# A convolution and maxout kernel: w10 from 16 products, four columns first added on VectorE, sums of one batch moved ahead

## Chip, cores, metric

One core of a Trainium2 chip. The sets of experiments (a; b and c; d to g) ran on three different chips, so kernels of different sets are compared by their ratios and not by their medians. Times are device microseconds (us) of a whole execution. A profiled execution also has a span, which is 1.8 us shorter than its time. Each kernel was timed in alternation with the kernel before on the same chip. A ratio is the mean time of one kernel's fast runs over that of the other's fast runs of the same rounds, so it is not quite the ratio of the medians quoted.

## The reference, cut to what matters

```python
w = softmax(weight_gen, over the 7 taps)          # 8 batches x 4160 rows x 8 heads x 7
y[b,s,h,g] = sum_k w[b,s,h,k] * x_pad[b,s+k,h,g]  # 7 taps, 24 values per head, 192 columns
h1 = y @ w1;  h2 = y @ w2                         # 192 -> 1024
out = maximum(h1, h2) @ w_out                     # 1024 -> 192
```

The kernel uses max(h1, h2) = h1 + relu(h2 - h1): `out = y @ (w1 @ w_out) + relu(y @ (w2 - w1)) @ w_out`. The small product `w10 = w1 @ w_out` is made once, at the start.

## The kernel before

The 33,280 rows are laid out as 260 columns of 128 rows. VectorE multiplies x by the seven weights and adds the taps (`mul`, `adds`). For the first columns TensorE does the adding, by seven products with an identity; for the others a transposing DMA brings the sum to TensorE.

```python
    def adds(b, o):
        ...
        nc.vector.tensor_tensor(out=taps(0, 1, 3), in0=taps(0, 1, 3), in1=taps(3, 1, 3), op=ALU.add)
        nc.vector.tensor_tensor(out=taps(0, 2, 2), in0=taps(0, 2, 2), in1=taps(1, 5, 2), op=ALU.add)
        nc.vector.tensor_tensor(out=y_ts[b][:, o * D:(o + w) * D], ...)

    def transpose(u):
        ...
        nc.sync.dma_start_transpose(out=yt[...], in_=y_ts[b][:, o * D:(o + n) * D])
        ...
            nc.gpsimd.tensor_copy(out=gate, in_=yt[:, 0:1])   # waits for the transpose, then loads x

    def sum_transpose(u):
        for k in range(nb):
            for t in range(K):                                # seven taps
                nc.tensor.matmul(yps[...], lhsT=m_ts[b][...], rhs=ident, start=(t == 0), stop=(t == K - 1), ...)
        nc.scalar.copy(out=yt[:, 0:nb * P], in_=yps[:, 0:nb * P])
```

Eight columns are a unit here. Each unit passes VectorE (product, three adds), a transpose, TensorE (`hd`, products with w2 - w1), ScalarE (`rd_t`, the relu), TensorE again (`op_ps`), ScalarE (`o_t`, the copy out) and a store.

The softmax here doesn't subtract the row's maximum and nothing guards it: scores larger than these inputs give would overflow.

## Time and profile before

428.1 us (427.99 to 428.15, three runs); with the fourth run beside the changed kernel (427.70) the median is 428.05.

| | before |
|---|---|
| span | 425.9 us |
| TensorE busy | 418.4 us, 98% |
| VectorE busy | 381.8 us, full from 30 us to 391.4 us |
| transposes of w1, products of w10 | 2.58 us, 1.98 us |
| last copy out starts, end | 422.16, 425.9 us |

The lines of the page and how they are read are in the prediction below. The end of the kernel before is shown here: the timeline of ScalarE (ACT), with start, duration, engine, line and what ended the idle time.

```profile
422.16 0.48 ACT L305 COPY o_t<-op_ps 128x384 f32<-128x384 f32 x1 [1.01 <-PE op_ps L292]
422.67 0.34 ACTq L312 DMA_DIRECT2D out_dram<-o_t  x1
```

One copy of the last two columns waits for TensorE, then one store follows; 3.74 us from the copy's start to the end.

### The profile page before, as it was taken

To read this page: it belongs to the slowest core of one execution; us is meant where nothing else is said; L and a number is where in the kernel's file an instruction comes from. 1 tells how busy PE (TensorE), PEld (TensorE's weight loads), DVE (VectorE), ACT (ScalarE), POOL (GpSimd) and SP (SyncE) were. 2 spreads that over 40 slices of the span, in tenths; PEclk is the share of its full clock that TensorE was granted. 3 is DMA by queue.
4 is the path that set the end of the run, shared out by engine and by line. 5 is a ranking of instruction groups with operands and counts; after the bars stand their busy time and mean duration, and the time that the engine had idled before them with its cause. 6 is when DMAs were issued, how large, how long until landed. Compare 5 with 4: busy or idle time off the path is not lost.

```text
span 425.9 us, 9277 instructions
## 1 busy us (share of the span) xinstructions
PE 418.4 (98%) x4139; PEld 300.2 (70%) x4139; DVE 381.8 (90%) x176; ACT 351.5 (83%) x353; POOL 81.5 (19%) x101
## 2 busy tenths in 40 slices
PE   7999999999999999999999999999999999999996
PEld 7889876666776767766667767667666677676685
DVE  6989999999999999999999999999999999997000
ACT  5896889898888979788898979898887988787762
POOL 1510032323112213221201131130222113110000
PEclk9999999999999999999999999999999999999999
DMA  8994256585675656667776667666766566644112
GB/s 253 252 233 93 76 145 150 86 198 168 169 191 112 202 130 184 159 130 192 175 193 124 161 159 184 138 165 179 178 154 182 96 162 149 154 115 131 75 75 111
DMA packets 62167, 65.85 MB, mean 155 GB/s; under 512 B 49937, under 2 KB 50577, under 8 KB 62128
## 3 DMA queue, kind: packets, MB, share of 16 engines
q0 software_dynamic: 8128, 24.11, 27.0%
q1 hardware_dynamic: 48672, 15.59, 18.7%
q10 hardware_dynamic: 5328, 25.56, 15.4%
q8 instruction: 32, 0.52, 0.5%
q14 instruction: 7, 0.06, 0.0%
HBM read 35.96 MB, written 25.56 MB: 144 GB/s over the span
## 4 chain that ended last, share of the span: by engine, by line
PE 94%; ACT 3%; DMA 2%; SPq 1%; issue 0%
PE op_ps L292 40%; PE hd L237 27%; PE hd L247 14%; PE op_ps L282 5%; PE op_ps L275 3%; PE yps L208 2%; DMA xs<-in_x_dram 2%; PE hdp L237 1%; ACT rd_t L256 1%; PE hdp L247 1%; PE tp L490 1%; SPq L426 1%; PE pw L533 0%; ACT en_t L146 0%; ACT o_t L305 0%; ACT xb_t L455 0%
## 5 line engine op out<-in xcount | busy, mean ns | idle before, releaser
L256 ACT ACTIVATE rd_t<-hd 128x2048 bf16<-128x2048 f32 (+1 forms) x166 | 230.9, 1445 | 33.1 <-PE hd L247 32.6
L292 PE MATMUL op_ps<-wo,rd_t 128*128 128x192 bf16 x2080 | 200.2, 246 | 0.0
L157 DVE TENSOR_TENSOR m_t<-xb_t,en_t 128x10752 bf16<-128x10752 bf16 (+1 forms) x36 | 187.3, 5206 | 1.7 <-ACT en_t L146 1.5
L292 PEld LDWEIGHTS <-rd_t 128*128 128x128 bf16 x2080 | 175.6, 98 | 9.2
L192 POOL CAST gate<-yt 128x1 f32<-128x1 bf16 x28 | 45.8, 1635 | 278.9 <-DMA yt<-y_t 278.9
L237 PE MATMUL hd<-yt,wdE 128*128 128x512 bf16 (+1 forms) x264 | 96.5, 370 | 0.2 <-ACT rd_t L256 0.2
L237 PE MATMUL hd<-yt,wdO 128*128 128x512 bf16 (+1 forms) x264 | 95.5, 366 | 0.0
L175 DVE TENSOR_TENSOR m_t<-m_t 128x4608 bf16<-128x4608 bf16 (+1 forms) x31 | 76.9, 2480 | 1.1
L305 ACT COPY o_t<-op_ps 128x384 f32<-128x384 f32 (+1 forms) x89 | 56.1, 630 | 25.9 <-PE op_ps L292 23.8
L247 PE MATMUL hd<-yt,wdR 64*128 64x512 bf16 (+1 forms) x528 | 68.0, 366 | 0.0
L282 PE MATMUL op_ps<-w,yt 128*128 128x192 bf16 x260 | 64.0, 246 | 0.0
L176 DVE TENSOR_TENSOR m_t<-m_t 128x3072 bf16<-128x3072 bf16 (+1 forms) x31 | 52.9, 1706 | 1.1
L247 PEld LDWEIGHTS <-wdR 64*128 64x128 bf16 x576 | 20.8, 94 | 44.8 <-issue 35.0
L237 PEld LDWEIGHTS <-wdE 128*128 128x128 bf16 x288 | 28.0, 97 | 29.0 <-issue 19.2
L146 ACT ACTIVATE en_t<-wg_t 128x896 bf16<-128x896 f32 (+1 forms) x36 | 34.2, 960 | 2.1 <-ACT o_t L305 2.1
L237 PEld LDWEIGHTS <-wdO 128*128 128x128 bf16 x288 | 28.2, 98 | 10.4 <-issue 0.7
L282 PEld LDWEIGHTS <-yt 128*128 128x128 bf16 x260 | 25.4, 98 | 9.6 <-issue 0.3
L177 DVE TENSOR_TENSOR y_t<-m_t 128x1536 bf16<-128x1536 bf16 (+1 forms) x31 | 28.9, 932 | 1.1
L275 PE MATMUL op_ps<-w,yt 64*128 64x192 bf16 x260 | 25.2, 243 | 0.2 <-ACT o_t L305 0.2
L275 PEld LDWEIGHTS <-yt 64*128 64x128 bf16 x260 | 12.8, 94 | 14.6 <-issue 0.7
L130 DVE TENSOR_REDUCE sum_t<-e_t 128x128 f32<-128x896 f32 (+1 forms) x17 | 17.6, 1038 | 2.3 <-ACT e_t L125 2.3
L125 ACT ACTIVATE e_t<-wg_t 128x896 f32<-128x896 f32 (+1 forms) x17 | 15.7, 925 | 3.9 <-DMA wg_t<-in_weight_gen_dram 2.3
(51 smaller groups left out, 161.7 us busy)
## 6 DMA issues: line engine op xcount, KB each, us to landing
out_dram<-o_t ACTq DMA_DIRECT2D x29, 768.0 KB, 3.8
xb_t<-in_x_dram POOLq DMA_DIRECT2D x28, 384.0 KB, 4.7
wg_t<-in_weight_gen_dram POOLq DMA_DIRECT2D x14, 448.0 KB, 5.1
xb_t<-xb_t POOLq DMA_DIRECT2D x16, 288.0 KB, 5.0
out_dram<-o_t ACTq DMA_DIRECT2D x6, 384.0 KB, 2.6
wg_t<-in_weight_gen_dram SPq DMA_DIRECT2D x2, 448.0 KB, 5.2
xs<-in_x_dram SPq DMA_DIRECT2D x2, 384.0 KB, 6.4
xb_t<-in_x_dram POOLq DMA_DIRECT2D x1, 768.0 KB, 10.4
```

The costliest lines, as they stand in the source:

```text
L146: nc.scalar.activation(out=_sub(en_ts[b], o * WGC * 2, [[2 * N, K], [2, N], [1, 2]]), in_=_sub(wg_ts[b], o * WGC, [[1, K], [K, N], [0, 2]] ...
L157: nc.vector.tensor_tensor(out=m_ts[b][:, K * o * D:K * (o + n) * D], in0=_sub(xb_ts[b], o * D, [[D, K], [1, n * D]]), in1=_sub(en_ts[b], o ...
L175: nc.vector.tensor_tensor(out=taps(0, 1, 3), in0=taps(0, 1, 3), in1=taps(3, 1, 3), op=ALU.add)
L176: nc.vector.tensor_tensor(out=taps(0, 2, 2), in0=taps(0, 2, 2), in1=taps(1, 5, 2), op=ALU.add)
L192: nc.gpsimd.tensor_copy(out=gate, in_=yt[:, 0:1])
L237: nc.tensor.matmul(hid_out(t, f, j), lhsT=wd[kind][:, f * P:(f + 1) * P], rhs=_sub(yt_ts[u], 2 * j * P, [[3 * P, w // P], [1, P]]), start= ...
L247: nc.tensor.matmul(hid_out(t, f, j), lhsT=wd["R"][r, f * P:(f + 1) * P], rhs=_sub(yt_ts[u][r, :], P, [[3 * P, w // P], [1, P]]), start=fir ...
L256: nc.scalar.activation(out=rd[:, k * 1024:(k + n) * 1024], in_=hd[:, at:at + n * 1024], func=AF.Relu)
L275: nc.tensor.matmul(op_out(c), lhsT=yt_ts[u][r, (3 * i + 1) * P:(3 * i + 2) * P], rhs=w10[r, 2 * D:3 * D], start=first, stop=False, skip_gr ...
L282: nc.tensor.matmul(op_out(c), lhsT=yt_ts[u][:, (3 * i + 2 * j) * P:(3 * i + 2 * j + 1) * P], rhs=w10[:, j * D:(j + 1) * D], start=False, s ...
L292: nc.tensor.matmul(op_out(c), lhsT=rd[:, k * 1024 + at:k * 1024 + at + P], rhs=wo[:, f * D:(f + 1) * D], start=False, stop=(f == FCH - 1), ...
L305: nc.scalar.copy(out=_sub(o_t[0], (k + 2 * q) % 24 * D, [[2 * D, w], [D, 2], [1, D]]), in_=_sub(tile_, at + q * D, [[D, w], [512, 2], [1, ...
```

## The change

It takes transposes and products off TensorE while w10 is made, has VectorE do the first of the adding steps of columns 16 to 19 so that TensorE sums four taps instead of seven, brings the softmax sums of batch 1 ahead of the last product of batch 0, splits the last copy and store over two engines, and moves later softmax work by a few tiles.

```diff
+        nc.vector.tensor_tensor(out=taps(0, 1, 3), in0=taps(0, 1, 3), in1=taps(3, 1, 3), op=ALU.add)
+        if first:
+            return
 ...
-            for t in range(K):
+            for t in taps:
 ...                                                     # in evac, for the last pair
+            for j, copy, eng in ((0, nc.scalar.copy, nc.scalar), (1, nc.vector.tensor_copy, nc.sync)):
+                copy(out=o_t[0][...], in_=tile_[:, at + j * 512:at + j * 512 + D])
+                eng.dma_start(...)
 ...                                                     # transposes of w1
-                for at, kind, nr in ((0, "E", P), (P + 64, "E", 64), (P, "T", 64)):
+                for at, kind, nr in ((0, "E", P), (P, "T", 64)):
 ...                                                     # the order
         mul(0, 8)
         sum_transpose(1)
-        mul(0, 12)
         exp_sum(1)
         red(1)
         hidden(1)
-        w1_transposed()
         ln(1)
         shift(1)
+        mul(0, 12)
+        w1_transposed()
+        weights(1, 0)
+        weights(1, 4)
 ...                                                     # w10
-            for k in range(3):
+            for at, c0, nr in ((0, 0, P), (512, P, 64)):
                 for fi in range(FCH):
                     nc.tensor.matmul(...)
-            nc.scalar.copy(out=_sub(w10, 0, [[D, 3], [1, D]]), in_=_sub(pw, 0, [[256, 3], [1, D]]))
+            for k, to, frm, at in ((0, 0, 0, 0), (1, 0, 64, 0), (2, 64, 0, 0), (1, 64, 0, 512), (2, 0, 0, 512)):
+                nc.scalar.copy(...)
 ...
         mul(1, 0)
+        adds(1, 0, True)
 ...
-        4: (lambda: (exp_sum(3), sum_transpose(4)), lambda: weights(2, 0)),
+        4: (lambda: (exp_sum(3), sum_transpose(4, (0, 1, 2, K - 1))), lambda: weights(2, 0)),
 ...
-        if s == 1 and b + 2 < NB:                        # ln, shift, mul, adds of later batches
+        if s == 4 and b + 2 < NB:
```

## The prediction

> **What bounds the kernel now.** I read the page's busy times and forty slices first, then the chain that ended last, then the timeline of each engine, then the landings of the transposing DMA.
>
> ```profile
> PE 418.4 (98%) x4139; PEld 300.2 (70%) x4139; DVE 381.8 (90%) x176; ACT 351.5 (83%) x353; POOL 81.5 (19%) x101
> ...
> PE   7999999999999999999999999999999999999996
> ...
> DVE  6989999999999999999999999999999999997000
> ...
> PE 94%; ACT 3%; DMA 2%; SPq 1%; issue 0%
> ```
>
> TensorE (PE) is busy from 3.0 us to the end, and 94% of the chain is TensorE. The reader should also see the DVE row: VectorE is full from 30 us until it has finished at 391.4 us. In the DVE timeline one half batch (8 columns) takes 12.05 us (y_t written at 61.60, 73.65, 85.69 us); in the PE timeline the first products of units three apart (131.06 and 167.11 us) lie 36.05 us apart, 12.02 us per half batch. So TensorE is the bound, but VectorE keeps exactly its pace, only some microseconds ahead of it.
>
> How far ahead is what limits this change. GpSimd's gate waits for each transpose, so its start shows the landing; I compare it with TensorE's first product on that unit.
>
> ```profile
> 189.46 1.88 POOL L192 CAST gate<-yt 128x1 f32<-128x1 bf16 x1 [11.76 <-DMA yt<-y_t]
> 210.06 2.77 POOL L192 CAST gate<-yt 128x1 f32<-128x1 bf16 x1 [7.77 <-DMA yt<-y_t]
> 246.18 2.78 POOL L192 CAST gate<-yt 128x1 f32<-128x1 bf16 x1 [8.17 <-DMA yt<-y_t]
> 298.11 1.62 POOL L192 CAST gate<-yt 128x1 f32<-128x1 bf16 x1 [12.00 <-DMA yt<-y_t]
> ```
>
> The first column is the start. TensorE needs these units at 190.9, 213.3, 249.4 and 299.0 us: slacks of 1.4, 3.2, 3.2 and 0.9 us. Of 28 units most have 2.5 to 3.3 us, some 4 to 5; the first and fourth above are the smallest. (The gate at 298.11 may overstate: the last data packets of that transpose ended 2 us before.)
>
> Between 20 and 45 us, where most of the change is:
>
> ```profile
> 23.21 1.93 ACT L496 COPY w1t<-tp 128x1024 bf16<-128x1024 bf16 x2 [0.52 <-PE tp L490]
> 31.39 0.69 ACT L539 CAST w<-pw 128x576 bf16<-128x576 f32 x1
> 25.38 1.09 DVE L138 TENSOR_TENSOR wg_t<-wg_t,sum_t 128x896 f32<-128x896 f32 x1 [0.64 <-ACT sum_t L133]
> 27.71 2.96 DVE L157 TENSOR_TENSOR m_t<-xb_t,en_t 128x5376 bf16<-128x5376 bf16 x1 [1.24 <-ACT en_t L146]
> 28.51 2.14 PE L533 MATMUL pw<-wo,w1t 128*128 128x192 bf16 x24
> 37.79 2.51 PE L208 MATMUL yps<-ident,m_t 128*128 128x128 bf16 x42
> 45.10 0.27 PE L237 MATMUL hd<-yt,wdE 128*128 128x256 bf16 x1 [0.23 <-ACT rd_t L256]
> ```
>
> ScalarE (ACT) has no gap from 23.2 to 32.1 us, VectorE has two, and TensorE waits 0.23 us for ScalarE at 45.1 us and 0.20 us at 50.8 us, then never again before the tail.
>
> **What the Trainium skill says.** "TensorE: Matmul & The Clock Gate", "Wait — 56ns, not 53.3ns?": back to back, a product costs its columns at 2.4 GHz plus about 2.5 ns, 55.6 ns for 128. The trace agrees: 42 products of 128 columns take 2.35 us (56 ns), 24 of 192 columns take 1.98 us (82.5 ns). "TensorEngine Tiling (Array Packing)", "Key Properties": changing the tiling mode drains TensorE. The trace agrees: among the transposes of w1 the weight loads come 0.15 us apart where 128 rows change to 64 or back, 0.03 us apart between two of 64 rows. "DMA: Bandwidth & Descriptors", "Issuing engines are not separate DMA queues": issuing from two engines saves only issue time; no run here shows it yet for the last store. The same page, "Queues, rings and completion order": a semaphore increment lands only after every earlier write of that DMA engine, across queues. The trace fits: where an output store is issued 0 to 1.15 us after y_t is ready, transposes land 5.7 to 7.7 us after it; where it comes 1.23 us or more after, 3.9 to 4.75 us.
>
> **The change part by part.**
>
> 1. *Transposes of w1, 24 to 16.* Before, eight chunks take 20.53 to 23.11 us, 0.32 each: two mode changes of 0.15 and one load of 0.03. The new pair keeps both mode changes, so only 8 x 0.03 = 0.25 us goes, not a third of 2.6.
> 2. *w10 products, 24 to 16.* 8 x 82.5 ns = 0.66 us; eight have 64 weight columns, which changes the tiling mode once or twice (estimate 0.1 us back). About 0.6 us.
> 3. *Copies on ScalarE.* w1t copies shrink by 2 x 256 elements at 0.83 ns (the slope between 384 and 768 elements, 0.48 and 0.80 us): -0.43 us. w10's one copy of 0.69 us becomes five of 192; back to back a copy costs its elements plus some 0.05 us (1024 elements start 0.905 us apart), so 0.21 each with 0.33 for the last: about +0.5 us. ln ahead of w1t fills the 0.52 us idle. Walking ScalarE's order with these starts, w10 is ready at 31.7 us; TensorE, 0.8 us early, asks for it at 32.1 us. No stall, but only 0.4 us to spare.
> 4. *Columns 16 to 19.* Four taps instead of seven: 18 of 42 products, 18 x 56 ns = 1.0 us off TensorE. VectorE gets one add of 1.36 us (what the same shape takes at 34.57 us). It ends at about 31.2 us and is asked for at 37.0 us: hidden.
> 5. *Sums of batch 1 ahead of the last product of 0.* Fills most of the two VectorE gaps: reduction at 20.9, subtraction 22.9 to 24.0, then products without waiting. The second product of batch 1 moves from 31.58 to about 32.15 us: 0.56 us later, the 1.4 us add less 0.8 us of gap. From there VectorE has no idle, so all its later work is 0.56 us later.
> 6. *Last pair.* Intended: two engines copy and two queues store. But the built program's waits show otherwise: ScalarE's copy waits for the last product of both columns and VectorE's copy waits for ScalarE's. So 0.33 + 0.3 us in a row (estimates) take the place of 0.48; the store is 96 KB instead of 192, worth some 0.15 us (192 KB land in 2.1, 384 in 2.6 us). Net 0, at worst +0.2.
> 7. *Later places* of ln, subtraction, weights: VectorE's order is unchanged, ScalarE's work the same. The tightest, the weights of batch 3, would be ready at about 73 us for a product at 75.1 us. Nothing.
>
> Sum on TensorE: 0.25 + 0.6 + 1.0 = 1.85 us. At 42 to 45 us ScalarE is on the chain: its order (copy of yt, copy out, weights, relu) can come forward by 1.5 us, where the copy of yt ends. So TensorE is 1.5 us early from 45 us on. It does not wait again in the trace before, so this carries to the end if nothing new waits: 428.1 - 1.5 = 426.6.
>
> **The rivals.**
>
> *A, it carries through*: 426.6 us. For it: 94% of the chain, no later waits; and where a store is issued just after y_t, moving it to well before y_t should shorten those landings, among them the two tightest.
>
> *B, VectorE and the transposes become the bound.* TensorE and the stores it sets off move 1.5 us forward, VectorE 0.56 us back: 2.1 us against slacks of 0.9 to 3.3. If no landing changes its latency, the unit at 299.0 us waits 1.2 us, and 0.3 us of gain is left: 427.8. A variant: for every third unit the store now comes 3.0 to 3.6 us after y_t; 2.1 less puts the late ones (from 242 us) under 1.15 us, where landings took 2 us longer, and 3.0 - 2.1 - 2.3 is a wait of 1.4 us: 428.0. Against it: the same shift takes the two tightest units out of the bad place.
>
> *C, ScalarE with five copies holds TensorE up at 32 us.* If each copy costs 0.33 us alone, w10 is ready at 32.2 to 32.4 us: 0.1 to 0.3 us lost, 426.9. And a *better A*, where the waits of 45 and 51 us go too: 1.85 + 0.4, 425.8.
>
> **Range and chances.** A about half, B or a part of it a third, C and the better A the rest. The middle of these is 426.8 us; 8 in 10 between 425.7 and 428.0. A change of 2% is 8.6 us; all the TensorE work touched is under 3 us, and the worst wait found is under 3, so within 2% gets 0.98, and 0.01 each side.
>
> **What would show it.** The page: PE products fewer by 34 (8 + 8 + 18). The transposes of w1 still about 2.3 us; the 16 products about 1.4 us; 24 products near 37 us in 1.34 us; no wait at op_ps near 32 us; first hd product of 256 columns near 43.6 us. VectorE's y_t of the first half batch at about 50.1 us. ScalarE's and VectorE's last copies one after the other. Under A no unit's first product waits for a transpose; under B the waits show one of 0.3 us or more for yt, and all TensorE time after it shifts. Wrong would be: a transposing pair well under 0.3 us, VectorE later by over 1 us, or TensorE idle above 1 us between 60 and 400 us.

## The result, and the profile after

The changed kernel took 427.0 us (426.37 to 427.49, four runs) against 428.05: ratio 0.9976, 95% interval 0.9959 to 0.9993. Six runs of a later set gave 426.79 us (426.52 to 426.95), ratio 0.9968. The profiled execution is the fastest of the first four, 426.37 us.

The page of the changed kernel: busy times, the slices of TensorE and VectorE, the chain by engine.

```profile
PE 416.6 (98%) x4105; PEld 298.2 (70%) x4105; DVE 383.6 (90%) x178; ACT 352.1 (83%) x357; POOL 89.7 (21%) x101
...
PE   7999999999999999999999999999999999999996
...
DVE  6999999999999999999999999999999999999000
...
PE 92%; ACT 4%; DMA 2%; SPq 1%; issue 1%; ACTq 0%; DVE 0%; DVEq 0%
```

34 products fewer, 1.8 us less of TensorE, two instructions and 1.8 us more on VectorE, whose dip between 21 and 32 us (the third slice) is gone. The timelines between 20 and 45 us:

```profile
23.09 1.50 ACT L508 COPY w1t<-tp 128x768 bf16<-128x768 bf16 x2
30.66 1.56 ACT L555 CAST w<-pw 128x192 bf16<-128x192 f32 x5
24.04 5.82 DVE L157 TENSOR_TENSOR m_t<-xb_t,en_t 128x5376 bf16<-128x5376 bf16 x2
29.89 1.36 DVE L173 TENSOR_TENSOR m_t<-m_t 128x2304 bf16<-128x2304 bf16 x1
28.39 1.60 PE L547 MATMUL pw<-wo,w1t 128*128 128x192 bf16 x16
37.23 1.50 PE L210 MATMUL yps<-ident,m_t 128*128 128x128 bf16 x24
43.85 0.27 PE L239 MATMUL hd<-yt,wdE 128*128 128x256 bf16 x1 [0.54 <-ACT rd_t L258]
```

ScalarE's copies, the add, the 16 and the 24 products stand where the prediction put them to some 0.3 us, except that the five copies end at 32.2 us and not at 31.7. TensorE now waits 0.54 us for ScalarE at 43.85 us, where it had waited 0.23. The ends, in the timelines of ScalarE, VectorE and the queue of SyncE:

```profile
420.85 0.32 ACT L307 COPY o_t<-op_ps 128x192 f32<-128x192 f32 x1 [1.00 <-PE op_ps L294]
421.26 0.36 DVE L307 COPY o_t<-op_ps 128x192 f32<-128x192 f32 x1 [29.28 <-ACT o_t L307]
421.65 0.36 SPq L308 DMA_DIRECT2D out_dram<-o_t  x1
```

VectorE's copy is released by ScalarE's copy and not by TensorE: the two run one after the other, and from 420.85 us to the end of the span (424.6) it is 3.75 us, as long as before.

The landings of the transposes, seen in GpSimd's gate (start first):

```profile
165.41 2.42 POOL L194 CAST gate<-yt 128x1 f32<-128x1 bf16 x1 [11.21 <-DMA yt<-y_t]
176.23 1.04 POOL L194 CAST gate<-yt 128x1 f32<-128x1 bf16 x1 [7.40 <-DMA yt<-y_t]
186.69 2.64 POOL L194 CAST gate<-yt 128x1 f32<-128x1 bf16 x1 [8.40 <-DMA yt<-y_t]
295.67 2.05 POOL L194 CAST gate<-yt 128x1 f32<-128x1 bf16 x1 [8.98 <-DMA yt<-y_t]
```

TensorE needs these units (its first weight load for them is due) at 165.8, 175.9, 189.6 and 297.7 us. The third and fourth are the two that were tightest before: they have 2.9 and 2.0 us now. The first two have 0.4 and -0.3 us: a weight load waited 0.3 us there, which TensorE's queued work hid. Over the 28 units the median slack fell from 2.84 to 1.66 us.

**Four stretches.** Four marks in TensorE's timeline cut an execution into parts that answer to different causes: the first transpose of w1, the first product `hd`, the start of the last eight products, the end of the span. All times in us; the last two columns are the median of the timed runs and the ratio to the kernel before.

| kernel | to transposes of w1 | to first hd | to last eight | to end | median | ratio |
|---|---|---|---|---|---|---|
| before | 20.53 | 24.57 | 376.20 | 4.60 | 428.05 | 1 |
| changed | 20.64 | 23.21 | 376.14 | 4.61 | 427.0 | 0.9976 |
| a1_again | 20.78 | 23.21 | 376.52 | 4.59 | 426.79 | 0.9968 |
| a2_vector_less | 20.27 | 23.23 | 376.13 | 4.57 | 426.27 | 0.9957 |
| a3_vector_more | 20.77 | 23.20 | 379.90 | 4.53 | 428.13 | 1.0001 |
| a4_vector_twice | 20.37 | 24.18 | 378.28 | 4.57 | 430.19 | 1.0057 |
| b1_seven_taps | 20.52 | 23.90 | 376.14 | 4.54 | 427.15 | 0.9984 |
| b3_old_w10 | 21.11 | 24.18 | 376.15 | 4.56 | 427.41 | 0.9989 |
| b5_old_order | 21.58 | 23.40 | 377.23 | 4.59 | 427.89 | 0.9998 |
| c1_own_banks | 20.35 | 23.21 | 376.93 | 4.41 | 427.14 | 0.9984 |
| d1_sums_earlier | 20.68 | 23.19 | 376.13 | 4.60 | 426.39 | 0.9963 |
| e1_exp_later | 20.38 | 22.90 | 376.67 | 4.55 | 427.21 | 0.9995 |
| g1_store_later | 20.67 | 22.95 | 380.44 | 4.64 | 430.89 | 1.0072 |
| f1_all | 21.08 | 22.94 | 376.48 | 4.40 | 426.59 | 0.9962 |

The last of the four is good to 0.05 us only, since the spans are given to 0.1 us. Each ratio has a 95% interval of 0.0012 to 0.0029 to either side, so ratios that differ by less than some 0.002 are not told apart by the times.

The first column scatters by over 1 us between executions of kernels that do the same there up to that point, or nearly so; differences of 0.3 us between single spans say nothing for that reason. The second column is the gain of the change: 24.57 - 23.21 = 1.36 us. The third is 376.13 to 376.20 us in every execution without a wait there; what is above that is waits and what they set off, and in c1 and f1 also a moved product of 0.26 us. The table has one profiled execution of each kernel, the medians come from four to seven.

### The profile page after: what moved, and what is told of

Read it like the earlier page. It is cut to its first block, busy times and chain, and to the rows that moved or that the text cites. A ratio compares the mean times of both kernels' runs of the same rounds, so it can differ in the third digit from the quotient of the medians.

```text
span 424.6 us, 9214 instructions
## 1 busy us (share of the span) xinstructions
PE 416.6 (98%) x4105; PEld 298.2 (70%) x4105; DVE 383.6 (90%) x178; ACT 352.1 (83%) x357; POOL 89.7 (21%) x101
## 4 chain that ended last, share of the span: by engine, by line
PE 92%; ACT 4%; DMA 2%; SPq 1%; issue 1%; ACTq 0%; DVE 0%; DVEq 0%
PE op_ps L294 39%; PE hd L239 27%; PE hd L249 14%; PE op_ps L284 5%; PE op_ps L277 3%; DMA xs<-in_x_dram 2%; PE yps L210 2%; ACT rd_t L258 2%; PE hdp L239 1%; PE tp L502 1%; PE hdp L249 1%; SPq L437 0%; ACT en_t L146 0%; ACT o_t L316 0%; ACT yt L216 0%
## 5 line engine op out<-in xcount | busy, mean ns | idle before, releaser
L194 POOL CAST gate<-yt 128x1 f32<-128x1 bf16 x28 | 54.7, 1955 | 272.4 <-DMA yt<-y_t 272.4
L173 DVE TENSOR_TENSOR m_t<-m_t 128x4608 bf16<-128x4608 bf16 (+1 forms) x32 | 78.2, 2445 | 1.1
```

## The experiments

### How much VectorE can be late

a1_again is the changed kernel. a3 and a4 add one or two adds of the same size on dead taps; a2 leaves the new add out (its four columns are wrong; relative error 0.075).

```diff
         if first:
+            nc.vector.tensor_tensor(out=taps(3, 1, 3), in0=taps(3, 1, 3), in1=taps(3, 1, 3), op=ALU.add)   # a3; twice in a4
             return
```

```diff
-        nc.vector.tensor_tensor(out=taps(0, 1, 3), in0=taps(0, 1, 3), in1=taps(3, 1, 3), op=ALU.add)       # a2
         if first:
             return
+        nc.vector.tensor_tensor(out=taps(0, 1, 3), in0=taps(0, 1, 3), in1=taps(3, 1, 3), op=ALU.add)
```

> The changed kernel unaltered, as the base for the others of this call and to see how far its executions scatter. Theory B (VectorE and the transposes hold TensorE up in some executions): 426.9 us median, and a scatter of about 1 us against 0.4 us for the kernel before. Theory A (TensorE's work alone): the executions agree within 0.4 us, near 426.5.

> The add of 1.36 us on VectorE is left out and TensorE still sums only four taps, so four columns come out wrong on purpose; TensorE's work is the same and VectorE is 1.36 us earlier from 31 us on. Theory A: the time of the changed kernel within 0.1 us. Theory B: 0.4 to 0.7 us faster, near 426.4, and the scatter falls to 0.4 us or less.

> A second add of the same 1.36 us on taps that nobody reads again follows the first; results stay right, TensorE's work is the same, VectorE is 1.36 us later from 31 us on. Theory A: the time of the changed kernel within 0.2 us. Theory B: 0.7 to 1.4 us slower, 427.6 to 428.3, with TensorE waiting for a transpose in the trace.

> Two such adds, VectorE 2.72 us later. Theory A with 2 us of slack left: 0.7 us slower than the changed kernel at most. Theory B: 2.0 to 2.7 us slower, 429.0 to 429.7, since each us of VectorE past the slack is a us of the end.

Measured on one chip: 426.27 (VectorE 1.36 us earlier), 426.79 (as changed), 428.13 (1.36 later), 430.19 us (2.72 later). TensorE's work is the same in all four, so the time follows VectorE: less steeply while there is slack left, by 0.5 us from a2 to a1, by 1.3 us from a1 to a3 and by 2.1 us from a3 to a4, each a step of 1.36 us. a4 is 0.5 us above the range expected of it (429.0 to 429.7); two of its six runs had a lower granted clock, see below. The scatter of a1 was 0.43 us and not 1, that of a2 (0.60) not smaller, and that of the kernel before 1.8 us in the same set and not 0.4: that part of the expectation failed, and scatter is no sign of the waits. In the waits of a1 there was this:

```profile
PEld L249 <- DMA yt<-y_t: 0.7, 1, 0.7
...
PE hd L249 <- DMA yt<-y_t: 0.2, 1, 0.2
```

Columns: total us, times, longest. One weight load waited 0.7 us for a transpose and TensorE 0.2 us. In a2 no such wait is listed, and its third stretch is 0.39 us shorter. The unit waited for is the one needed at 176 us, and it is the same unit that is waited for in c1, e1 and b5 below. It landed 5.7 to 6.6 us after its y_t in these executions, while most others whose store comes at the same place landed after 4.0 to 4.7 us; why this one is slow is open.

a3's profiled execution (430.22 us, its slowest) showed more than was looked for. In TensorE's timeline, and below it four stretches from 104 to 112 us (busy times of the engines, then the granted clock PEclk):

```profile
106.32 0.39 PE L250 MATMUL hd<-yt,wdR 64*128 64x512 bf16 x2 [1.93 <-ACT rd_t L259]
```

```profile
104.00:106.00 2.00, 0.39 (x4) 0.00 (x0) 2.00 (x1) 1.64 (x2) 0.00 (x0) 1.00 0.70 133
106.00:108.00 2.00, 1.68 (x14) 1.14 (x15) 1.97 (x2) 0.86 (x2) 1.25 (x3) 0.84 0.00 0
108.00:110.00 2.00, 2.00 (x15) 1.90 (x13) 1.97 (x2) 0.47 (x1) 0.00 (x0) 0.50 0.88 88
110.00:112.00 2.00, 2.00 (x21) 1.93 (x19) 1.97 (x3) 0.00 (x0) 0.00 (x0) 0.80 0.95 257
```

The wait is put down to ScalarE, but a weight load just before waited 2.4 us for the transpose: that unit landed 6.57 us after y_t. After the idle 1.93 us the granted clock fell to half. From the shares 0.84, 0.50 and 0.80 the fall began at about 107.4 us, 1.0 us after the wait had ended, and lasted 3.4 us. So the wait cost twice: the third stretch is 3.8 us over its floor (376.14 us). In a4 two gaps came without a fall of the clock:

```profile
44.55 0.27 PE L241 MATMUL hd<-yt,wdE 128*128 128x256 bf16 x1 [1.51 <-ACT rd_t L260]
106.94 0.39 PE L251 MATMUL hd<-yt,wdR 64*128 64x512 bf16 x2 [1.59 <-DMA yt<-y_t]
```

The first of them is in its second stretch: TensorE waited for ScalarE, which stood behind the later VectorE.

The record has the mean granted clock of every run, profiled or not. 3.4 us at half clock lower it by 0.004 (estimate: 3.4 / 2 / 428). It is 0.998 or more in every profiled run without such a fall, and 0.996 in a3's slowest run. The other runs at 0.996 or less are a4's two slowest, e1's slowest and all six of g1: those lost time to the clock too.

### The parts undone

```diff
-        adds(1, 0, True)                                     # b1_seven_taps
-        4: (lambda: (exp_sum(3), sum_transpose(4, (0, 1, 2, K - 1))), ...
+        4: (lambda: (exp_sum(3), sum_transpose(4)), ...
```

> Columns 16 to 19 are summed from seven taps on TensorE again and VectorE's add of 1.36 us is gone; all else as changed. TensorE has 18 products (1.0 us) more, of which 0.54 us falls into its present wait for ScalarE at 43.9 us, and VectorE is 1.36 us earlier. By TensorE's work alone: 0.5 to 1.0 us slower than the changed kernel, 427.3 to 427.8. With VectorE's lead deciding part: the waits for transposes go, so about 427.1 to 427.3, as good as the changed kernel within 0.4 us, and with a small scatter.

427.15 us, inside the second expectation. In the profile its second stretch is 0.69 us longer than the changed kernel's (1.0 us of products, of which 0.3 went into a shorter wait for ScalarE) and the third stands on its floor: with VectorE 1.36 us earlier no transpose was waited for. The add that saves TensorE 0.7 us takes from VectorE's lead.

```diff
-                for at, kind, nr in ((0, "E", P), (P, "T", 64)):             # b3_old_w10: w10 as before
+                for at, kind, nr in ((0, "E", P), (P + 64, "E", 64), (P, "T", 64)):
 ...                                                          # and 24 products, one copy
```

> Transposes, products and copies of w10 as before (24, 24, one copy), all else as changed. In the profiles the new ones saved 0.23 us of transposes and 0.44 us of products. By TensorE's work alone: 0.67 us slower than the changed kernel, about 427.5. With VectorE's lead deciding part, TensorE arrives 0.67 us later at units where it had 0 to 0.7 us to spare: about 0.4 us slower, 427.2, with less scatter.

427.41 us: slower, nearer to the first expectation. The second stretch is 0.97 us longer, 0.67 from the shorter pieces as expected and 0.3 from TensorE's small waits before the w10 products, where the longer w1t copies hold ScalarE's relus back.

```diff
+        mul(0, 12)                                           # b5_old_order: where it was
         exp_sum(1)
         red(1)
         hidden(1)
+        w1_transposed()
         ln(1)
         shift(1)
-        mul(0, 12)
-        w1_transposed()
-        weights(1, 0)                                        # after hidden(2), as before
-        weights(1, 4)
```

> Sums of batch 1 after the last product of batch 0 again, all else as changed: TensorE's work is the same, VectorE's two gaps come back (0.6 and 1.2 us before, 0.3 and 0.9 us in the changed kernel), so VectorE is some 0.7 us later. By TensorE's work alone: no change. With VectorE's lead deciding: 0.5 to 0.9 us slower than the changed kernel, 427.3 to 427.8.

427.89 us, 0.9998 of the kernel before: with the old order the rest of the change is worth nothing. TensorE's work is unchanged and the second stretch loses only 0.19 us, 0.13 us of it a wait for w10's copies; the third is 1.1 us over its floor, and TensorE waited 0.9 us for a transpose at one unit:

```profile
178.43 0.39 PE L249 MATMUL hd<-yt,wdR 64*128 64x512 bf16 x2 [0.91 <-DMA yt<-y_t]
```

The order costs about what theory B expected of it (0.9 to 1.3 us by the ratios, 0.5 to 0.9 expected). But VectorE is only 0.38 us later here and not 0.7 (its second product of batch 1, counted from the first transpose of w1), and the unit that was waited for landed 6.60 us after its y_t, against 5.66 us in the changed kernel. In this execution, then, most of the wait is a longer landing; that VectorE's order makes it longer is not shown.

### The last pair

```diff
+                own = ps["ab"].tile([P, 2048], FP32, name="ab_last", tag="ab")   # c1_own_banks
+                op_at[c // 2] = own, -512
+                out_rest(c, True)                            # the last column's own first product
             out_col(c)
```

> The last two columns get a PSUM tile each, so ScalarE's copy waits for the first column's products alone and VectorE's copy for the second's, not for ScalarE's copy. If the serial copies are what the last pair gained nothing by: VectorE's copy starts 0.35 to 0.4 us earlier after the last product and the whole is 0.3 to 0.4 us faster than the changed kernel. If the store's landing sets the end whatever starts it: no change.

427.14 us; no gain, but for neither reason. VectorE's copy is now released by TensorE:

```profile
421.50 0.36 DVE L397 COPY o_t<-ab_last 128x192 f32<-128x192 f32 x1 [29.79 <-PE ab_last L294]
421.89 0.36 SPq L398 DMA_DIRECT2D out_dram<-o_t  x1
```

Read along the chain, TensorE's end to the store's issue took 421.33 to 421.89, 0.56 us, where the changed kernel took 420.83 to 421.65, 0.82 us. That is 0.26 us gained. But the last column's 64-row product, moved between two groups of 128 rows, made TensorE 0.26 us longer. Its third stretch is 0.79 us over the floor: this product, and what a transpose waited for at 176.4 us cost (0.3 us of idle time). So the serial copies were what the last pair gained nothing by, and this mending costs as much as it saves.

### Room for VectorE, ScalarE's wait, the stores

```diff
         nc.scalar.copy(out=w1["E"], in_=ws["E", 0])
+        exp_sum(1)                                           # d1_sums_earlier
 ...
+        red(1)
         mul(0, 8)
         sum_transpose(1)
-        exp_sum(1)
-        red(1)
-        hidden(1)
         ln(1)
         shift(1)
+        hidden(1)
         mul(0, 12)
```

> Exponentials, reduction and logarithm of batch 1 still earlier: the exponentials before the first relu, the reduction before and the subtraction after the third product of batch 0. The order on TensorE is unchanged; VectorE's two gaps of 0.29 and 0.94 us should go, so VectorE is 1.2 us earlier from 25 us on, with right results. VectorE's lead deciding: 0.4 to 0.6 us faster than the changed kernel, near 426.3, as when the add was left out. TensorE's work alone: no change.

426.39 us (426.26 to 426.76), ratio 0.9963, right results. y_t of the first half batch is ready at 49.15 us against 50.14 in the changed kernel (their starts were alike: transposes of w1 at 20.68 and 20.64 us), so VectorE is 1.0 us earlier; no wait for a transpose, third stretch on its floor. Its median is the lowest of the correct kernels. By the times alone a gain over the changed kernel is not shown, since a1's ratio is 0.9968 and the intervals overlap; the profile shows what went away.

```diff
-        4: (lambda: (exp_sum(3), sum_transpose(4, ...)), ...                     # e1_exp_later
-        5: (none, lambda: transpose(6)),
+        4: (lambda: sum_transpose(4, ...), ...
+        5: (none, lambda: (exp_sum(3), transpose(6))),
```

> The exponentials of batch 3 move from ahead of the relu at 37 us to after the copy out at 44 us, where ScalarE waited 1.3 us. TensorE's wait of 0.54 us at 43.9 us should go, so TensorE is 0.5 us earlier from there and VectorE unchanged. TensorE's work alone: 0.5 us faster than the changed kernel. VectorE's lead deciding: the 0.5 us are lost again at the next late transpose, no gain to 0.2 us, with TensorE waiting for yt in the trace.

427.21 us (426.31 to 430.79; the slowest run has a mean granted clock of 0.996, and the profiled one is the fastest). The second stretch fell by 0.31 us (TensorE's wait from 0.54 to 0.2), and the third grew to 0.54 us over its floor, with two weight loads waiting 1.2 us in all for transposes. In this execution, as theory B has it, what TensorE gained it lost at the next late transposes.

```diff
+        while pending:                                       # g1_store_later: the store of the copy before
+            pending.pop(0)()
 ...
-                nc.scalar.dma_start(...)
+                if u < NU - 2: pending.append(store)
+                else: store()
```

> Each store of 8 columns is issued one copy later (some 4 us), except the last ones; engines' work is the same. In the changed kernel stores issued from 0.7 us before to 1.6 us after y_t went with landings of 5.7 to 6.9 us; now nearly all should come 2 us or more after y_t. If collision with the stores makes the late landings: every landing 5.0 us or less, no wait of TensorE for yt, 0.3 to 0.6 us faster than the changed kernel. If the store has nothing to do with them: landings and time as before, within 0.2 us.

430.89 us: a miss. Most of it went as expected: the median landing fell from 4.73 to 4.26 us after y_t, the median slack rose from 1.66 to 2.75 us. But four units landed late, at 5.6, 6.1, 6.2 and 9.15 us. The last of these, in TensorE's timeline and in the stretches 300 to 302, 302 to 304 and 304 to 306 us:

```profile
300.12 0.38 PE L240 MATMUL hd<-yt,wdE 128*128 128x512 bf16 x1 [2.10 <-DMA yt<-y_t]
...
302.47 1.48 PE L295 MATMUL op_ps<-wo,rd_t 128*128 128x192 bf16 x8
```

```profile
300.00:302.00 2.00, 1.88 (x12) 0.66 (x12) 1.97 (x2) 0.71 (x1) 1.25 (x3) 0.88 0.16 9
302.00:304.00 2.00, 2.00 (x13) 1.59 (x12) 1.97 (x3) 2.00 (x2) 0.00 (x0) 0.50 0.77 83
304.00:306.00 2.00, 2.00 (x13) 1.28 (x11) 2.00 (x2) 0.82 (x3) 0.00 (x0) 0.77 1.02 264
```

TensorE waited 2.10 us, and the clock was then half for 3.4 us, from 1.4 us after the wait: eight products that take 0.82 us took 1.48. In the packet records the transpose's data took 6.6 us instead of some 2, with the store's packets coming in 1.4 us after its first ones. The store had been issued 1.3 us after y_t, and the transpose itself 0.56 us after it, where 0.15 is usual. Here a store that began in the middle of a transpose went with the longest landing of all these profiles (the next is 8.32 us, in b1). But of five others whose store came 1.1 to 1.4 us after y_t four landed after 4.3 to 4.4 us and one after 6.1, so the place of the store alone does not decide. Why this unit and not its like is open. The other five runs were not profiled, but their mean granted clocks (0.991 to 0.995) say that each had at least one such fall.

> The three above together and the two PSUM tiles for the last columns. If the causes are right they add: 0.5 us of TensorE's wait at 43.9 us and 0.2 to 0.3 us at the end, with VectorE's lead and the landings giving room for both and for the 0.5 us that waits cost: 425.4 to 425.8 us. If room is not what lacked: 426.5 or more.

426.59 us (425.85 to 426.76), ratio 0.9962: slower than expected, and no better than d1 alone. With VectorE 1.0 us earlier, the same later stores came at least 1.8 us after y_t, landings were 3.9 us in the median and 6.34 at most, and TensorE waited for no transpose. The 0.5 us hoped for at the first hd were 0.27 (g1 alone has 0.27 and e1 alone 0.31, so they do not add), the end gained 0.2 and its own product cost 0.26, and the profiled execution had begun 0.4 us late.

## Why the prediction was right

It said 426.8 and the kernel takes 427.0, or 426.79 in the second set. That it came so near is in part luck: 426.8 was the middle of two theories, 426.6 and 427.8 to 428.0, and the first four runs lie between 426.37 and 427.49. Step by step:

- **What bounds it**: right. TensorE sets the time until VectorE's lead is used up; a2, a1, a3 and a4 show the second half, with TensorE's work unchanged.
- **Transposes of w1**: 0.25 us said, 20.64 to 22.99 us is 2.35 instead of 2.58, which gives 0.23. Both mode changes stayed, as said. (One reading was off: two loads of 64 rows come 0.015 to 0.02 us apart and not 0.03, and a chunk went from 0.323 to 0.295 us.)
- **Products of w10**: about 0.6 us said, 1.98 to 1.54 gives 0.44. The term that was mis-sized is "changes the tiling mode once or twice (estimate 0.1 us back)": it measured 0.22, two changes of some 0.1 each at the ends of the eight products.
- **Copies on ScalarE**: no stall was right, the sum was short. Five copies took 1.56 us, not 1.17 (three of the four that follow another start 0.32 to 0.38 us after it, only one 0.22), and ended at 32.2 us, with TensorE asking at 32.4: 0.16 us to spare, not 0.4. Rival C did not happen, but narrowly; in b5 TensorE did wait, 0.13 us.
- **Columns 16 to 19**: 24 products took 1.35 us (1.34 said), the add was done 6 us before it was asked for. Undone, 0.69 us came back, the rest fell into ScalarE's wait, as the sum on TensorE had it.
- **Sums ahead, VectorE 0.56 us later**: 32.17 against 31.58 us for the second product of batch 1, 0.59.
- **Sum on TensorE**: 1.5 us said, 1.36 measured in the stretch up to the first hd, the same to 0.02 us in five other executions. The 0.14 us are about the mis-sized mode change (0.12): it comes before the relu at 37.2 us, from which ScalarE works without a gap until TensorE waits for it at 43.85.
- **Last pair**: right, net 0 (3.74 and 3.75 us), and by the reason given: two copies in a row, shown by c1.
- **Rivals**: the answer lay between A and B, as the middle figure assumed. The profiled execution is A; in the one of a1, the same kernel, B has begun (0.4 us over the floor), and a3, a4 and e1 show more of it with VectorE 1.36 us later or TensorE 0.3 us earlier. B's variant was not reached: the stores moved by 1.9 us and not 2.1, so none came within 0 to 1.15 us after y_t, and those at 1.2 to 1.7 us landed at 4.2 to 4.5 us, with one at 4.9 and one at 5.7. Late (6.7 to 6.9 us) were three units whose store came 0.4 to 0.7 us before y_t, which no rival named; two others in that place landed at 4.8 and 5.0 us. The rule of "0 to 1.15 us after y_t" was read from one arrangement, and g1 shows that it isn't a rule.
- **Not foreseen**: that a wait of about 2 us is followed by a fall of the clock to half (a3, g1), so the worst cases cost twice.

What stays open: the changed kernel's three other runs of the first set took 0.5 to 1.1 us more than the profiled one. Starts that scatter and waits for transposes both can do that; a fall of the clock did not, since their mean granted clock is 1.0. Those executions were not profiled.

## What to carry to other kernels

Before work is moved off the busiest engine, measure how far ahead of it its supplier runs, unit by unit: an engine with 90% busy may have 1 us of lead, and a saving larger than the lead turns into a wait. When two engines are that close, room for the second one has a price too: here VectorE 1.36 us earlier gained 0.5 us (a2), and 1.36 us later cost 1.3 us (a3). And two copies meant to run side by side should be looked up in the built program's waits: out of one tile, the second was released by the first here.

## What the Trainium skill lacked or had wrong

- "TensorE: Matmul & The Clock Gate", Part 1 and "Why this matters for your kernels": puts the fall to half clock at an idle window of about 3.4 us and warns of gaps over some 3 us. Here gaps of 1.93 and 2.10 us were followed, 1.0 and 1.4 us after their end, by a granted clock of 0.50 for 3.4 us; gaps of 1.51 and 1.59 us were not. Two cases each make no new threshold.
- "TensorEngine Tiling (Array Packing)", "Key Properties": says that a change of mode drains TensorE, not what it costs. Here weight loads come 0.13 to 0.16 us apart between transposes of 128 and 64 rows, one 64-row product moved between groups of 128 rows made TensorE 0.26 us longer (c1), and the two changes around eight products of 64 weight columns cost 0.22 us.
- "DMA: Bandwidth & Descriptors": no section has the size of what stores do to a DMA transpose beside them. The same transpose of 8 columns landed 3.94 us after its data was ready in the median where stores began at least 1.8 us after it (f1), and up to 9.15 us (g1) with a store of 768 KB.
